# A WKV recurrence with a soft mixture of experts: scores on four quarters of the array, and the bonus sums with r*k as the stationary operand

## The chip, the cores and the metric

The kernel runs on one core of a Trainium2 chip. The metric is the device time in microseconds (us) of one execution. The engines are PE (TensorE: matmuls, with its weight loads listed apart as PEld), DVE (VectorE), ACT (ScalarE), POOL (GpSimd) and SP (SyncE, which issues the DMAs). All data is float32, and a float32 matmul stands in the trace as two weight loads and two matmuls (two passes); a transpose of float32 stands as one of each.

## The reference

A recurrence over 768 tokens for 4 batches of 8 heads of size 48, followed by a soft mixture of experts over the 3072 tokens of width 384.

```python
def _attn_ref(r, k, v, w, u):
    B, H, S, D = r.shape                      # 4, 8, 768, 48
    state = np.zeros((B, H, D, D))
    for t in range(S):
        cur = np.einsum('bhd,bhe->bhde', u[None] * kt, vt)
        y[:, :, t] = np.einsum('bhd,bhde->bhe', rt, state + cur)
        state = wt[:, :, :, None] * state + np.einsum('bhd,bhe->bhde', kt, vt)

def _moe_ref(x, phi, w1, w2):                 # 8 experts with 4 slots each
    logits = x @ phi
    d = softmax of logits over the tokens     # slot_input = d.T @ x
    slot_out[e] = np.maximum(slot_input[e] @ w1[e], 0.0) @ w2[e]
    c = softmax of logits over the slots
    return c @ slot_out
```

The term with `u` is a scalar for each token and head, a = sum over d of r*k*u, times v. The kernel computes it apart from the rest. Its tensor `rk` holds r*k with the head's rows along the partitions and the tokens along the free axis, and `u_sb` holds u in a few columns.

## The kernel before

The recurrence is cut into chunks of 128 tokens (C = 6 for a sequence). A *unit* is a load of 128 partitions: two heads of 48 rows at partitions 0 and 64, and below each of them 16 rows that are a third of a further head. Three loaded units (NU = 3) so hold the data of four pairs of heads, and the fourth pair (its rows gathered by small DMAs into `k3` and `r3`) is worked on like the others. There are 4 batches of 4 pairs, so NIT = 16 pairs, and a software pipeline runs over `it` from 0 to 16: in step `it` the pair n = it - 1 is computed, the results of pair m = it - 2 are taken from PSUM and fed to the mixture, and the scans for later units are made.

The order on each engine is that of the code (a schedule by hand). In a step PE does, one after the other:

- transposes of the keys (`tp`, L298; five matmuls, not for the fourth pair), which ACT copies to `kn` (L299, L302);
- `b_scores` (L313): for each of six chunks and each of two heads one matmul of keys against queries. The 48 rows of a head lie at array rows 0 or 64, all 128 key columns are the stationary operand, and the 128 tokens of the queries stream. It goes in two halves of three chunks. The result `ap` (a bank for each head) is copied by ACT to `at` (L317) and masked by POOL (L318);
- `d_a` (L252), in steps in which a unit is prepared (`A`, it % 4 < 3): u is stationary in three column groups of 32, and r*k streams with 256 tokens for each. The result [96, 256] is copied by ACT to `aT` (L255);
- `b_u` (L329): the chunks' contributions to the state (`up`), which DVE scans into `Sb` (L335) and ACT copies to `Sn` (L338);
- transposes of the finished results of pair m (`tp`, L384), copied by ACT to `xT` (L386), not in every step;
- `c_av` (L350): masked scores against v, with a stationary operand of 128 rows by 64 columns;
- `d_a_turn` (L260): two transposes of `aT`, so that the tokens lie along the partitions; ACT copies the result to `a` (L263);
- the mixture's logits `lp` (L401), in one step in four its sums `sp` (L448) and its transposes `dp` and `ln` (L438, L471);
- `c_inter` (L365): queries against `Sn`, on quarters of the array (48 rows by 64 columns), into the same `y` as `c_av`.

DVE does the decay scans (L206 and L218) with the products around them (L217, L220), the scan of the state (L335) and the evacuation of `y` plus `av` into `x` (L375). POOL makes `rk` (L244), the masks and `av` (L284: v times `a`, for the next step). SP loads the inputs of later units (`ld`, `rt`, `vt`) and, in pieces, the expert weights (`wt`).

The PSUM tiles of `d_a`, `d_a_turn`, the scores and the transposes come from one pool of four banks (`ps_t`, tag `tp`). Behind step 16 follow the mixture's sums and the two expert layers (L536, L572) and the output (L601).

Of the kernel before, what the change touches and what calls it, by code (L numbers as in the profile page):

```python
# [9 lines left out]
F32 = mybir.dt.float32  # L10
# [9 lines left out]
P = 128  # L20
# [21 lines left out]
NU = 3  # L42

NL = 4
PART = 16

HALF = 3

E1 = P + 1
# [4 lines left out]
def rwkv_soft_moe(ctx: ExitStack, tc: tile.TileContext, wkr, v, ublk, phi, w1, w2, out_a, out_b):  # L54
    nc = tc.nc
# [3 lines left out]
    C = v.shape[3]  # L59
# [16 lines left out]
    small = ctx.enter_context(tc.tile_pool(name="small", bufs=2))  # L76
# [13 lines left out]
    ps_t = banks.enter_context(tc.tile_pool(name="ps_t", bufs=4, space=PSUM))  # L90
# [6 lines left out]
    def a_load(i, lo=0, hi=R_OFF):  # L97
        nc.sync.dma_start(out=lds[i % NL][:, lo:hi], in_=wkr[i, :, lo:hi])

    def a_load_r(i, lo=0, hi=SCAN):  # L100
        nc.sync.dma_start(out=rts[i % NL][:, lo:hi], in_=wkr[i, :, R_OFF + lo:R_OFF + hi])
# [10 lines left out]
    ident = const.tile([P, P], F32, name="ident")  # L112
# [9 lines left out]
    NTG = 3  # L122
    TG = NTG * NS
# [3 lines left out]
    u_sb = const.tile([P, NG, 32], F32, name="u_sb")  # L127
# [34 lines left out]
    rks = [decay.tile([P, S], F32, name=f"rk{n}") for n in range(2)]  # L162
# [16 lines left out]
    def keys(i):  # L179
        return by_chunk(lds[i % NL][:, K_OFF:R_OFF])[:, :, 1:E1]  # L180
# [14 lines left out]
    parts, a3 = {}, {}  # L195
    xb = {}

    def a_load_v(i):
        vt = vpool.tile([P, 2, C, D], F32, name="vt")
        nc.sync.dma_start(out=vt, in_=v[i])  # L200
        sts[i]["vv"] = vt
# [27 lines left out]
    def a_gather(i):  # L229

        lo = PART * (i % NU)
        for dst, src in ((k3, lds[i % NL][:, K_OFF:R_OFF]), (r3, rts[i % NL])):
            for h in range(2):
                nc.sync.dma_start(out=dst[64 * h + lo:64 * h + lo + PART], in_=src[64 * h + D:64 * h + 64])

# [10 lines left out]

    def d_a(i):

        ap = ps_t.tile([TG, 2, P], F32, name="aps", tag="tp")
        rkc = rks[i % 2].rearrange("p (c e) -> p c e", e=P)  # L250
        for j in range(NTG):
            nc.tensor.matmul(out=ap[32 * j:32 * j + 32], lhsT=u_sb[:, i % NU, :], rhs=rkc[:, j:C:NTG, :],  # L252
                             start=True, stop=True)
        parts[i] = aT = small.tile([TG, 2, P], F32, name="aT", bufs=1)
        nc.scalar.copy(out=aT, in_=ap)  # L255

    def d_a_turn(i):
        tp = ps_t.tile([P, 2, P], F32, name="atp", tag="tp")
        for n in range(2):
            nc.tensor.transpose(out=tp[:, n, 0:TG], in_=parts[i][:, n, :], identity=ident[0:TG, 0:TG])  # L260

        parts[i] = a = small.tile([P, 4, C, 1], F32, name="a", bufs=5)
        nc.scalar.copy(out=a.rearrange("p h (n j) o -> p h n (j o)", n=2),  # L263
                       in_=tp[:, :, 0:TG].rearrange("p n (j q) -> p q n j", q=32)[:, 0:4])

    def d_a_last(b):
        a3[b] = t = small.tile([P, 2, C, 1], F32, name="a3")
# [4 lines left out]
    def unit(i):  # L272
        return NU * (i // NG) + i % NG

    def rows_of(i):
        if i % NG == NU:
            return k3, r3
        return lds[unit(i) % NL][:, K_OFF:R_OFF], rts[unit(i) % NL]
# [7 lines left out]
    def b_kn(i, hf):  # L286
# [6 lines left out]
        kn, kv = st["kn"], keys(unit(i))  # L293
        at3 = PART * (i % NG)
        lo, hi = ((0, 3), (3, C - 1))[hf]
        tp = ps_t.tile([P, 3, P], F32, name="tp")
        for c in range(lo, hi):
# [4 lines left out]
        nc.scalar.copy(out=bass.AP(tensor=dst.tensor, offset=dst.offset + at3,  # L302
                                   ap=[dst.ap[0], dst.ap[1], [64, 2], [1, PART]]), in_=src)

    def b_scores(i, hf):
        st = sts[i]
        kt_, rt_ = rows_of(i)
        aps = [ps_t.tile([P, 3, P], F32, name="ap", tag="tp") for _ in range(2)]
        order = [(cc, h) for cc in range(3) for h in range(2)]
        for cc, h in order:  # L310
            c = 3 * hf + cc
            rows = slice(64 * h, 64 * h + D)
            nc.tensor.matmul(out=aps[h][:, cc, :], lhsT=kt_[rows, c * E1 + 1:(c + 1) * E1],  # L313
                             rhs=rt_[rows, c * E1:c * E1 + P], start=True, stop=True)
        for h in range(2):
            at = work.tile([P, 3, P], F32, name="at")
            nc.scalar.copy(out=at, in_=aps[h])  # L317
            nc.gpsimd.affine_select(  # L318
                out=at, in_=at, pattern=[[0, 3], [1, P]], compare_op=ALU.is_gt,
                fill=0.0, base=0, channel_multiplier=-1)  # L320
            st["AT", h, hf] = at
# [291 lines left out]
    def recompute():  # L613
# [5 lines left out]
        with tc.tile_pool(name="f_dram", bufs=1, space=DRAM) as f_dram, \  # L619
# [17 lines left out]
            with tc.For_i(0, B, 1) as ib:  # L637
              for g in range(NG):
                for h in range(2):
# [186 lines left out]
    for it in range(NIT + 1):  # L826
        n, m = it - 1, it - 2
        ph = it % NG
        A, i = it < NIT and ph < NU, unit(it)
        B_ = n >= 0  # L830
        mb, mg = divmod(m, NG)
        X = m >= 0 and mg >= 1
        Y = mg == 0 and mb >= 1
        Z = mg == 1 and mb >= 1
        U_ = B_ and n % NG < NU

        done = i if it == 0 or (A and ph) else unit(it + 1) if ph == NU and it + 1 < NIT else None
        if U_:
            a_gather(unit(n))
        if 1 <= it < NIT - 1:  # L840
            a_load_v(it + 1)
        if m >= 0 and m % NG < NU and unit(m) + NL < NSC:
            a_load(unit(m) + NL)
            a_load_r(unit(m) + NL)
        if it < NIT:
            more_weights(it)
        if it == NIT:
            early.close()
            late = weights.enter_context(tc.tile_pool(name="late", bufs=1, side="right", reuse_waits="tile"))
            w_b = weights.enter_context(tc.tile_pool(name="w_b", bufs=N_WB, side="right", reuse_waits="tile"))  # L850
            load_weight(w_b, wts, N_WB)
            cT = late.tile([P, NT // NB, P], F32, name="cT")
            siT = late.tile([P, E * KT, NS], F32, name="siT")
            nc.gpsimd.memset(siT, 0.0)
        if it == 0:
            masks()
            d_rk(0)
            scans(0, (("G", 0), ("F", 0), ("G", 1), ("F", 1)))
            d_a(0)
            d_a_turn(0)  # L860
            keep_warm(N_WARM_2[0], ps_t, "tp")
            d_rk(1)
        if ph == NU:
            d_a_last(it // NG)
        if B_:
            d_av(n)
            b_kn(n, 0)
            if n:
                b_kn(n, 1)
            b_scores(n, 0)  # L870
            if not n:
                keep_warm(N_WARM_2[1], ps_t, "tp")
                b_kn(n, 1)
        if m >= 0:
            c_evac(m)
        if it != 1:
            pieces_of(it, FIRST)
        if B_:
            b_scores(n, 1)
        if A and it:  # L880
            d_a(i)
        if B_:
            b_u(n)
        if Y:
            s_exp(mb - 1, qs[mb - 1])
        if X:
            xT = l_turn(xb[mb], mg - 1, once, ps_t)
            if mg == 1:
                lts[mb] = small.tile([TG, 2, P], F32, name="lt", bufs=1)
        if B_:  # L890
            if not U_:
                spread(pat3, k3)
            b_state(n)
        if Z:
            s_norm(mb - 1, qs[mb - 1])
        if it == 1:
            d_rk(2)
            pieces_of(it, FIRST)
        pieces_of(it, SECOND)

        if ph == NU - 1 and it + 2 < NIT:
            d_rk(i + 1)
        elif ph == NU and it + 1 < NIT:
            d_rk(done + 1)
        elif A and ph == 0 and it:
            d_rk(i + 2)
        if it == 1:
            keep_warm(N_WARM_2[2], ps_t, "tp")
        if B_:
            c_y(n)  # L910
            c_av(n, 0)
            c_av(n, 1)
        if A and it:
            d_a_turn(i)
        if X:
            l_part(mg - 1, xT, lts[mb], ps_t)
        if done is not None:
            a_pat(done)
            a_end(done)
        if X and mg == NG - 1:  # L920
            qs[mb] = s_max(mb, lts[mb], cst[0:TG, 2:3])
        if Y:
            s_dturn(qs[mb - 1], ps_t)
            s_rows(qs[mb - 1], ps_t)
            s_rows_exp(qs[mb - 1])
        if Z and mb < B - 1:
            s_slots(xb[mb - 1], mb - 1, qs[mb - 1], ps_t)
        if it == 1:
            keep_warm(N_WARM_2[3], ps_t, "tp")
        if B_:  # L930
            c_inter(n, 0)
            c_inter(n, 1)
        if Z and mb < B - 1:
            s_sum(mb - 1, qs[mb - 1])
# [21 lines left out]
    q = s_max(lb, lp)  # L956
# [162 lines left out]
```

## Time and profile before

| | |
|---|---|
| median of three runs | 188.88 us (186.36, 188.88, 191.8) |
| profiled execution, time of its own | 189.19 us |
| its span | 187.4 us |
| mean granted TensorE clock | 0.975 |
| PE, DVE, ACT, POOL busy | 88%, 65%, 48%, 41% |

The steps of the recurrence fill the span from about 6 to 136 us; the expert layers and the output take the rest. A group row of the profile gives the line, the engine and the operation, output<-inputs, shapes and count, then the busy time and the mean duration of one, then the idle time ahead of it and what ended that. Matmuls of different parts of the array overlap, so the time of a run of them is read from the chain of waits or the timeline, not from the mean of one. "issue" is idle time that ended on nothing that the trace shows.

### The profile page before, as it was taken

How to read it: one execution, taken by the hardware profiler on the slowest of the kernel's cores; microseconds unless marked ns; L12 is line 12 of the kernel's file. 1: busy time of each engine (PE TensorE's matmuls, PEld its weight loads, DVE VectorE, ACT ScalarE, POOL GpSimd, SP SyncE). 2: the span in 40 equal slices, each digit the busy share in tenths (PEclk: the TensorE clock that was granted, in tenths of full speed). 3: DMA queues.
4: the chain of work that ended last, by engine and by line, in shares of the span. 5: the costliest groups of instructions: out<-in, count | busy, mean ns of one | idle time of the engine just before them, and what ended most of it. 6: DMA issues, size and time to landing. Idle time of an engine off the chain costs nothing.

```text
span 187.4 us, 7253 instructions
## 1 busy us (share of the span) xinstructions
PE 165.8 (88%) x3000; PEld 116.6 (62%) x3000; DVE 121.5 (65%) x237; ACT 90.8 (48%) x266; POOL 76.5 (41%) x133
## 2 busy tenths in 40 slices
PE   7499979799999889999899999899789999999710
PEld 2166758677878758688777787787554324755510
DVE  5599978867897977989799889731335222033520
ACT  3054547455677726667765586784450002022430
POOL 3357286572448567445577643557004000000000
PEclk9999999969999999999999999999999999999985
DMA  5999599995779999389999259497999159907692
GB/s 148 339 396 358 116 388 328 357 406 193 230 224 366 323 397 346 75 238 319 299 368 390 53 169 285 117 330 249 418 320 415 73 167 415 417 17 294 261 385 94
DMA packets 14249, 51.93 MB, mean 277 GB/s; under 512 B 2304, under 2 KB 3200, under 8 KB 13568
## 3 DMA queue, kind: packets, MB, share of 16 engines
q1 hardware_dynamic: 14208, 51.38, 77.3%
q8 instruction: 26, 0.43, 0.9%
q14 instruction: 15, 0.12, 0.2%
HBM read 44.28 MB, written 4.72 MB: 261 GB/s over the span
## 4 chain that ended last, share of the span: by engine, by line
PE 48%; DVE 27%; DMA 7%; ACT 7%; issue 5%; POOL 1%; SPq 0%; ACTq 0%; DVEq 0%; POOLq 0%
PE ap L313 9%; DVE cst L218 6%; PE hp L536 6%; PE so L572 6%; DVE cst L206 5%; DMA rt<-in_wkr_dram 5%; PE y L365 5%; DVE Sb L335 4%; DVE ld L217 3%; PE tp L384 3%; PE op L601 3%; PE up L329 3%; ACT Sn L338 3%; PE tp L298 3%; PE sp L448 3%
## 5 line engine op out<-in xcount | busy, mean ns | idle before, releaser
L318 POOL TENSOR_SCALAR_AFFINE_SELECT at<-at 128x384 f32<-128x384 f32 x64 | 31.2, 523 | 28.7 <-ACT at L317 28.7
L317 ACT COPY at<-ap 128x384 f32<-128x384 f32 x64 | 26.4, 490 | 6.8 <-PE ap L313 5.6
L350 PE MATMUL y<-vt,at 128*64 128x48 f32 x768 | 25.5, 223 | 0.0
L350 PEld LDWEIGHTS y<-vt,at 128*64 128x64 f32 x768 | 23.7, 138 | 2.3 <-POOL at L318 1.7
L284 POOL TENSOR_TENSOR av<-vt,a 128x576 f32<-128x576 f32 x16 | 18.5, 1154 | 13.7 <-ACT a L263 13.7
L218 DVE TENSOR_TENSOR_SCAN cst<-ld,cst 128x387 f32<-128x387 f32 x24 | 23.2, 968 | 0.8
L313 PE MATMUL ap<-rt,ld 48*128 48x128 f32 x288 | 22.8, 286 | 0.7 <-issue 0.7
L206 DVE TENSOR_TENSOR_SCAN cst<-ld,cst 128x387 f32<-128x387 f32 x24 | 22.9, 953 | 0.8 <-DMA ld<-in_wkr_dram 0.6
L244 POOL TENSOR_TENSOR rk<-rt,ld 128x384 f32<-128x384 f32 x24 | 20.3, 868 | 7.3 <-DMA rt<-in_wkr_dram 4.1
L313 PEld LDWEIGHTS ap<-rt,ld 48*128 48x128 f32 x288 | 20.1, 187 | 2.2 <-issue 1.3
L335 DVE TENSOR_TENSOR_SCAN Sb<-up,pat 112x288 f32<-112x288 f32 x16 | 12.1, 753 | 11.9 <-ACT pat L224 7.4
L375 DVE TENSOR_TENSOR x<-y,av 128x576 f32<-128x576 f32 x16 | 12.1, 756 | 8.9 <-PE y L365 8.9
L338 ACT COPY Sn<-Sb 112x240 f32<-112x240 f32 x16 | 10.1, 629 | 12.2 <-DVE Sb L335 12.2
L386 ACT COPY xT<-tp 128x384 f32<-128x384 f32 x24 | 10.3, 482 | 9.0 <-PE tp L384 9.0
L217 DVE TENSOR_TENSOR ld<-ld,cst 128x387 f32<-128x387 f32 x24 | 13.0, 542 | 2.2 <-POOL rk L244 2.2
L365 PE MATMUL y<-Sn,rt 48*64 48x48 f32 x480 | 10.1, 222 | 4.6 <-ACT Sn L338 2.7
L365 PEld LDWEIGHTS y<-Sn,rt 48*64 48x64 f32 x480 | 8.4, 134 | 9.4 <-issue 3.6
L299 ACT COPY kn<-tp 128x336 f32<-128x336 f32 (+1 forms) x24 | 9.6, 401 | 8.9 <-PE tp L298 8.7
L220 DVE TENSOR_TENSOR rt<-rt,cst 128x387 f32<-128x387 f32 x24 | 13.4, 558 | 0.8
L329 PEld LDWEIGHTS up<-vt,kn 128*48 128x48 f32 x320 | 8.8, 128 | 7.0 <-issue 5.8
L572 PE MATMUL so<-wt,hT 128*32 128x208 f32 (+1 forms) x256 | 12.5, 329 | 0.0
L384 PE MATMUL tp<-ident,x 128*128 128x128 f32 x72 | 10.9, 289 | 1.0 <-DVE x L375 1.0
(130 smaller groups left out, 241.9 us busy)
## 6 DMA issues: line engine op xcount, KB each, us to landing
wt<-in_w_dram SPq DMA_DIRECT2D x24, 512.0 KB, 7.1
ld<-in_wkr_dram SPq DMA_DIRECT2D x11, 775.0 KB, 6.4
wt<-in_w_dram SPq DMA_DIRECT2D x5, 1536.0 KB, 9.0
vt<-in_v_dram SPq DMA_DIRECT2D x16, 288.0 KB, 4.9
rt<-in_wkr_dram SPq DMA_DIRECT2D x11, 387.0 KB, 5.9
wt<-in_w_dram SPq DMA_DIRECT2D x3, 832.0 KB, 6.4
out_dram<-wt SPq DMA_DIRECT2D x3, 832.0 KB, 3.9
wt<-in_w_dram SPq DMA_DIRECT2D x3, 704.0 KB, 10.1
```

The lines of the kernel that those rows point to most:

```text
L206: nc.vector.tensor_tensor_scan(out=prod[:, ::-1], data0=t[:, lo + 1:lo + 1 + HALF * E1][:, ::-1], data1=one, initial=1.0, op0=ALU.mult, op ...
L217: nc.vector.tensor_tensor(out=k_, in0=k_, in1=prod, op=ALU.mult)
L218: nc.vector.tensor_tensor_scan(out=prod, data0=lds[i % NL][:, lo:lo + HALF * E1], data1=big, initial=1.0, op0=ALU.mult, op1=ALU.min)
L244: nc.gpsimd.tensor_tensor(out=rks[i % 2].rearrange("p (c e) -> p c e", e=P)[:, part], in0=queries(i)[:, part], in1=keys(i)[:, part], op=AL ...
L284: nc.gpsimd.tensor_tensor(out=av, in0=st["vv"], in1=a.broadcast_to([P, 2, C, D]), op=ALU.mult)
L313: nc.tensor.matmul(out=aps[h][:, cc, :], lhsT=kt_[rows, c * E1 + 1:(c + 1) * E1], rhs=rt_[rows, c * E1:c * E1 + P], start=True, stop=True)
L317: nc.scalar.copy(out=at, in_=aps[h])
L318: nc.gpsimd.affine_select(out=at, in_=at, pattern=[[0, 3], [1, P]], compare_op=ALU.is_gt, fill=0.0, base=0, channel_multiplier=-1)
L335: nc.vector.tensor_tensor_scan(out=Sb[0:ROWS].rearrange("p e n -> p (e n)"), data0=up[0:ROWS].rearrange("p e n -> p (e n)"), data1=(pat3 i ...
L350: nc.tensor.matmul(out=st["y"][cols, h, c * D:(c + 1) * D], lhsT=st["AT", h, hf][:, cc, cols], rhs=st["vv"][:, h, c, :], start=(c == 0), s ...
L365: nc.tensor.matmul(out=st["y"][cols, h, c * D:(c + 1) * D], lhsT=t[rows, c * E1 + 64 * th:c * E1 + 64 * th + 64], rhs=Sn[rows, c - 1, :], ...
L572: nc.tensor.matmul(out=so[32 * g:32 * g + NS, :], lhsT=hT[ft // 2][:, ft % 2, e, :], rhs=wts[E + e][:, base + ft * wd:base + (ft + 1) * wd ...
```

## The change

Scores: each matmul's stationary operand is cut into two halves of 64 columns, so that a matmul takes 48 rows by 64 columns of the array (a quarter) and writes 64 of the 128 partitions of its bank. The 128 tokens of the queries stream as before, now twice for each chunk and head. There are 24 matmuls in a step in place of 12.

Sums: r*k becomes the stationary operand, in pieces of 64 tokens, and four columns of u stream. The result has the tokens along the partitions at once, so `d_a_turn` and the copy to `aT` go, and `a` is copied in `d_a`. There are 12 matmuls in place of 3, and no transposes.

```diff
     def d_a(i):
 
-        ap = ps_t.tile([TG, 2, P], F32, name="aps", tag="tp")
-        rkc = rks[i % 2].rearrange("p (c e) -> p c e", e=P)
-        for j in range(NTG):
-            nc.tensor.matmul(out=ap[32 * j:32 * j + 32], lhsT=u_sb[:, i % NU, :], rhs=rkc[:, j:C:NTG, :],
-                             start=True, stop=True)
-        parts[i] = aT = small.tile([TG, 2, P], F32, name="aT", bufs=1)
-        nc.scalar.copy(out=aT, in_=ap)
-
-    def d_a_turn(i):
...
+        ap = ps_t.tile([P, C, 4], F32, name="aps", tag="tp")
+        for c in range(C):
+            for th in range(2):
+                nc.tensor.matmul(out=ap[HP * th:HP * th + HP, c, :],
+                                 lhsT=rks[i % 2][:, c * P + HP * th:c * P + HP * th + HP],
+                                 rhs=u_sb[:, i % NU, 0:4], start=True, stop=True)
         parts[i] = a = small.tile([P, 4, C, 1], F32, name="a", bufs=5)
-        nc.scalar.copy(out=a.rearrange("p h (n j) o -> p h n (j o)", n=2),
-                       in_=tp[:, :, 0:TG].rearrange("p n (j q) -> p q n j", q=32)[:, 0:4])
+        nc.scalar.copy(out=a.rearrange("p h c o -> p c (h o)"), in_=ap)
...
-        order = [(cc, h) for cc in range(3) for h in range(2)]
-        for cc, h in order:
+        for cc, th, h in [(cc, th, h) for cc in range(3) for th in range(2) for h in range(2)]:
             c = 3 * hf + cc
             rows = slice(64 * h, 64 * h + D)
-            nc.tensor.matmul(out=aps[h][:, cc, :], lhsT=kt_[rows, c * E1 + 1:(c + 1) * E1],
+            k0 = c * E1 + 1 + HP * th
+            nc.tensor.matmul(out=aps[h][HP * th:HP * th + HP, cc, :], lhsT=kt_[rows, k0:k0 + HP],
                              rhs=rt_[rows, c * E1:c * E1 + P], start=True, stop=True)
...
-        if A and it:
-            d_a_turn(i)
```

On PE, in the step of the fourth pair of a batch, the row is this before (line, instruction, output<-inputs, columns of the stationary by columns of the moving operand, and how many in a row):

```order
L365 MATMUL y<-Sn,rt_103 64x48 x20
L313 MATMUL ap<-r_138,k_137 128x128 x12
L252 MATMUL aps<-rk_134,u_sb 32x256 x3
L329 MATMUL up<-vt,kn_139 48x48 x10
L384 MATMUL tp<-ident,x 128x128 x6
L350 MATMUL y<-vt,at 64x48 x24
L260 MATMUL atp<-ident,aT 128x96 x2
L401 MATMUL lp<-xT,phi_sb 32x256 x3
L365 MATMUL y<-Sn,r_138 64x48 x20
```

And this now, with the lines of the changed file (seven lower from `b_scores` on):

```order
L358 MATMUL y<-Sn,rt_103 64x48 x20
L306 MATMUL ap<-r_138,k_137 64x128 x24
L253 MATMUL aps<-u_sb,rk_134 64x4 x12
L322 MATMUL up<-vt,kn_139 48x48 x10
L377 MATMUL tp<-ident,x 128x128 x6
L343 MATMUL y<-vt,at 64x48 x24
L394 MATMUL lp<-xT,phi_sb 32x256 x3
L358 MATMUL y<-Sn,r_138 64x48 x20
```

The scores have 24 rows in place of 12 and the sums 12 in place of 3; the two transposes between `c_av` and the logits are gone, and nothing else has moved.

On ACT, the next step (a first pair of a batch) reads thus before:

```order
L317 COPY at<-ap 128x384 x4
L255 COPY aT<-aps 96x256
L386 COPY xT<-tp 128x384 x2
L338 COPY Sn<-Sb 112x240
L263 COPY a<-atp 128x24
L224 COPY pat_136<-ld_100 128x48x5
```

And thus now:

```order
L310 COPY at<-ap 128x384 x4
L257 COPY a<-aps 128x6x4
L379 COPY xT<-tp 128x384 x2
L331 COPY Sn<-Sb 112x240
L225 COPY pat_136<-ld_100 128x48x5
```

The copy to `a` has moved from behind `Sn` to the place of the copy to `aT`, which is gone. The instructions of DVE, POOL and SP are the same in number and order.

More of the change, by code (lines that the diff above doesn't have):

```diff
@@ L45 @@
 PART = 16
+HP = P // 2
 HALF = 3
@@ L247, in d_a @@
     def d_a(i):
-        ap = ps_t.tile([TG, 2, P], F32, name="aps", tag="tp")
-        rkc = rks[i % 2].rearrange("p (c e) -> p c e", e=P)
-        for j in range(NTG):
-            nc.tensor.matmul(out=ap[32 * j:32 * j + 32], lhsT=u_sb[:, i % NU, :], rhs=rkc[:, j:C:NTG, :],
-                             start=True, stop=True)
-        parts[i] = aT = small.tile([TG, 2, P], F32, name="aT", bufs=1)
-        nc.scalar.copy(out=aT, in_=ap)
-    def d_a_turn(i):
-        tp = ps_t.tile([P, 2, P], F32, name="atp", tag="tp")
-        for n in range(2):
-            nc.tensor.transpose(out=tp[:, n, 0:TG], in_=parts[i][:, n, :], identity=ident[0:TG, 0:TG])
+        ap = ps_t.tile([P, C, 4], F32, name="aps", tag="tp")
[4 more added lines that the diff above has]
+                                 rhs=u_sb[:, i % NU, 0:4], start=True, stop=True)
         parts[i] = a = small.tile([P, 4, C, 1], F32, name="a", bufs=5)
-        nc.scalar.copy(out=a.rearrange("p h (n j) o -> p h n (j o)", n=2),
-                       in_=tp[:, :, 0:TG].rearrange("p n (j q) -> p q n j", q=32)[:, 0:4])
+        nc.scalar.copy(out=a.rearrange("p h c o -> p c (h o)"), in_=ap)
     def d_a_last(b):
@@ L859, in rwkv_soft_moe @@
             d_a(0)
-            d_a_turn(0)
             keep_warm(N_WARM_2[0], ps_t, "tp")
```

## The prediction

> **What bounds the kernel now.** The page first: its engine line, its two lines by slices of 4.7 us, the instruction queue, and the shares of the chain of waits.
>
> ```profile
> PE 165.8 (88%) x3000; PEld 116.6 (62%) x3000; DVE 121.5 (65%) x237; ACT 90.8 (48%) x266; POOL 76.5 (41%) x133
> PEclk9999999969999999999999999999999999999985
> DMA  5999599995779999389999259497999159907692
> q8 instruction: 26, 0.43, 0.9%
> PE 48%; DVE 27%; DMA 7%; ACT 7%; issue 5%; POOL 1%; SPq 0%; ACTq 0%; DVEq 0%; POOLq 0%
> ```
>
> PE carries the chain, DVE comes second, and PE has by far the most instructions: 6000 of about 6640. "q8" brought 26 packets of 0.43/26 MB = 16.5 kB. The third thing to see is the 5% of "issue", idle time that nothing in the trace ends. So I read the timeline of PE at such a hole, and then the counts of instructions from hole to hole (view by stretches; matmuls and weight loads counted apart).
>
> ```profile
> 36.27 0.45 PE L365 MATMUL y<-Sn,rt 48*64 48x48 f32 x15 [1.21 <-issue]
> 62.76 0.27 PE L313 MATMUL ap<-rt,ld 48*128 48x128 f32 x1 [0.71 <-issue]
> 69.20 0.32 PE L365 MATMUL y<-Sn,rt 48*64 48x48 f32 x5 [0.68 <-issue]
> 99.82 1.41 PEld L313 LDWEIGHTS ap<-r,k 48*128 48x128 f32 x22 [0.29 <-issue]
> 130.14 0.27 PE L313 MATMUL ap<-r,k 48*128 48x128 f32 x1 [0.43 <-issue]
> ...
> core 0: us, PE busy (x) PEld busy (x) DVE busy (x) ACT busy (x) POOL busy (x), PEclk, DMA share, GB/s
> 36.26:62.76 26.50, 25.25 (x501) 20.41 (x502) 21.28 (x37) 17.19 (x53) 13.84 (x23) 0.94 0.84 291
> 62.76:69.18 6.42, 5.75 (x128) 3.95 (x127) 5.82 (x13) 3.17 (x8) 4.37 (x7) 1.00 1.01 371
> 69.18:99.82 30.64, 29.74 (x626) 23.61 (x626) 26.59 (x48) 19.74 (x58) 17.92 (x29) 1.00 0.84 283
> 99.82:130.13 30.31, 29.10 (x628) 23.98 (x629) 21.91 (x40) 20.55 (x62) 16.30 (x29) 1.00 0.67 216
> ```
>
> The holes stand in the middle of runs of equal matmuls (after 25 of 40, after 35 of 40, ahead of the last of 24), so no semaphore explains them. Between them lie 1003, 255, 1252 and 1257 instructions: 4, 1, 5 and 5 times 256, less some semaphore instructions that the counts leave out. [...] I read this as PE running out of instructions: at every 256th the next packet has to be there. When is it asked for? The DMA view of two stretches behind such a boundary, one under load, one not (the second boundary is found by counting 256 on from 69.18):
>
> ```profile
> q1 hardware_dynamic: 392, 1.45, 99.1%
> ...
> q8 instruction: 1, 0.02, 5.8%
> ...
> 69.18:76.04 6.86, 6.60 (x124) 5.10 (x126) 5.40 (x8) 3.96 (x10) 3.61 (x7) 1.00 0.86 314
> ...
> q8 instruction: 1, 0.02, 5.9%
> ```
>
> The first row is 62.76 to 66.85: the DMA engines are full and no instruction packet moves. The second is 66.85 to 67.9: there it is, and PE goes on at 69.20, 1.3 us behind it. The boundary at 76.04 finds a quiet queue: its packet lies between 77.0 and 78.0 (last row). So a packet is asked for when the one before is opened, and takes 69.20 - 62.76 = 6.4 us under load, some 2.0 + 1.3 = 3.3 us without. 93.91 to 99.82 is 256 instructions and one more fetch that was waited for: 5.9 us.
>
> ```profile
> 93.91:99.82 5.91, 5.82 (x134) 4.08 (x130) 5.71 (x12) 3.17 (x7) 4.57 (x8) 1.00 1.00 375
> ```
>
> [...]
>
> **The change part by part.** The direct terms come from these rows, of the chain in order of time and of the groups:
>
> ```profile
> 44.50 0.80 PE y L365 x40
> 45.30 0.70 PE tp L298 x5
> 46.00 1.75 PE ap L313 x24
> 47.75 0.56 PE aps L252 x6
> 48.31 0.61 PE up L329 x20
> ...
> 64.42 1.53 PE y L350 x48
> ...
> 145.37 2.71 PE hp L536 x24
> ...
> L350 PEld LDWEIGHTS y<-vt,at 128*64 128x64 f32 x768 | 23.7, 138 | 2.3 <-POOL at L318 1.7 <-issue 0.6
> L313 PEld LDWEIGHTS ap<-rt,ld 48*128 48x128 f32 x288 | 20.1, 187 | 2.2 <-issue 1.3 <-ACT ce L481 0.5 <-ACT kn L302 0.2
> L260 PE MATMUL atp<-ident,aT 96*128 96x96 f32 x24 | 4.6, 274 | 0.5 <-ACT aT L255 0.5
> L255 ACT COPY aT<-aps 96x256 f32<-96x256 f32 x12 | 4.6, 380 | 7.1 <-PE aps L252 7.1
> L263 ACT COPY a<-atp 128x24 f32<-128x24 f32 x12 | 2.1, 175 | 3.4 <-PE atp L260 3.4
> ```
>
> *Scores on quarters.* L536 streams 512 columns on four column groups, one per 2.71/24 = 113 ns, so a group needs 4 x 113 = 452 ns, 0.88 ns a column, and 128 columns need 113 ns. The scores before are 12 rounds of two: 12 x 0.113 = 1.36 us, and two starts of some 0.2 us make the 1.75. After the change they are 12 rounds of four, and that four quarters do run at once is seen in L365 (0.80/40 = 20 ns each, for 48 columns that stream 42 ns). The rounds stay at 113 ns, so nothing is won in the stream. What is won is the first weight load of each half, 187 - 138 = 0.05 us, of which one half a step is free (the other waits for ACT's copies of `kn` to clear a bank), and, in the four steps without L298, the empty 0.15 us between L365 and the scores, which now have the same shape: 16 x 0.05 + 4 x 0.15 = 1.4 us, two thirds of it on the chain: -0.9.
>
> *Sums.* 12 matmuls are 24 passes with a stationary operand like that of L350, 1.53/48 = 32 ns each: 0.77 us for 0.56, +0.2 us in eleven steps, less some 0.07 for the shape that L329 shares. The chain passes L252 in four of them: +0.5. `rk` from POOL is due at the same place as before.
>
> *The turn that goes.* Two transposes, about 0.3 us of PE with their start, stand behind L350, where PE goes on to wait for `Sn` (the row below: 6.6 us in 8 times). They are hidden, and gain nothing now; if PE comes late they are 0.3 us of slack. Should that cover go, the price is 11 x 0.3 = 3.3 us at most. ACT loses the copy of 380 ns; it is busy 48% and no `Sn` waits for it: hidden. `a` is ready earlier by the stretch from L252 to L260, which ends POOL's wait for it; `av` is needed only a step later by L375: nothing. The bank of `atp` comes free, and banks only turn sooner. SP's queue holds the same DMAs.
>
> ```profile
> PEld y L365 <- ACT Sn L338: 6.6, 8, 1.5
> ...
> 20.00:56.00 36.00, 33.27 (x686) 26.56 (x686) 29.77 (x51) 21.43 (x63) 18.65 (x32) 0.95 0.83 285
> 56.00:76.00 20.00, 18.04 (x391) 14.20 (x391) 16.91 (x30) 12.18 (x36) 13.00 (x22) 1.00 0.96 345
> 84.00:104.00 20.00, 19.35 (x410) 15.53 (x401) 18.53 (x36) 13.71 (x42) 13.54 (x24) 1.00 0.93 330
> 121.00:136.00 15.00, 13.26 (x321) 11.01 (x313) 4.71 (x9) 9.03 (x25) 7.29 (x12) 1.00 0.89 321
> ```
>
> *More instructions.* Scores add 24 passes a step, so 48 instructions; the sums add 36 and the turn takes 4 away. In 16 steps that is 16 x 48 + 12 x 32 = 1152 on 6000, all of them between 10 and 135 us, where they are a quarter more: 4.5 packets. Under load (the 9s of the DMA line) lie about 19 us from 23 to 42, and the last three rows. From 56 to 76 PE has 782 instructions; two steps' scores (96), one of sums (36) and two turns (-8) make 906, 3.5 packets, in the 20 - 1.4 = 18.6 us that it runs: 5.2 us a packet. The two rows below it give 4.9 (212 more instructions) and 5.1 (96 more) in the same way. The supply is 6.4 and 5.9, say 6.2: each packet fetched under load comes 1.2 us late. About 14 packets are opened there, and the fetch of the first in each of the four stretches starts in a short queue: 10 x 1.2 = 12 us of holes. The five holes before are 3.3 us. More holes: 8.7 us.
>
> Not all of them are on the path. With three packets in two steps, the boundaries fall in turn into L365, L350 and L313. A hole in L350 first eats the wait for `Sn`, 6.6/8 = 0.8 us, and the 0.3 us of the turn: 3.3 holes lose 1.1 each, 3.6 us. So 8.7 - 3.6 = +5.1. From below it is nothing (every hole meets a wait), from above 8.7. I take 4.9: the 5.1, less a little for a hole that falls where DVE has the chain (27% of it).
>
> Sum: -0.9 + 0.5 + 4.9 = +4.5 us on the profiled execution's 189.19: 193.7. That execution lies 0.3 above the median of the runs shown (188.88), so the forecast is 193.4.
>
> **The rivals.**
> - *The holes are covered.* They would have to meet PE's waits for `Sn` or DVE's scans three times in four: 8.7/4 - 0.4 = +1.8, so 190.7. For it speaks that DVE has 27% of the chain; against it that all five holes shown lie inside L313 and L365, where PE waits for nothing else. It decides where less than 4.2 us of the 8.7 get through: then it is not slower.
> - *Fetches are hidden after all*: the holes have another cause that more instructions don't multiply. Then the direct terms stand alone, 188.88 - 0.4 = 188.5. For it speaks that only 5 of the 26 packets are followed by a hole, against it the multiples of 256. [...]
> - *Quarters stream faster.* Were the 113 ns of a round set by the load of 128 columns and not by the stream, a round would drop to L365's 4 x 20 = 80 ns: 12 x 0.033 = 0.4 us a step, 16 steps, -6 us, and with the holes at their lower end 182.5. L536 speaks against it: its weight loads have 32 columns, and a column still costs 0.88 ns.
> - *The clock.* The one 6 in PEclk, at 37 to 42 us, follows the longest hole (1.21 us). A second such stretch, of longer holes, would cost about 2 us more, and the holes at their upper end with it: 189.2 + 8.7 + 2 = 199.9.
>
> **How the numbers follow.** Late packets on the path as priced: 0.48. Covered holes: 0.28. Fetches hidden: 0.11. Faster quarters: 0.06. The clock as well: 0.07. About 2% (3.8 us) is what a measurement of this kernel can tell from no change. So slower is 0.48 + 0.07 = 0.55, the same 0.28 + 0.11 = 0.39, faster 0.06. The time is the likeliest case's, 193.4. The range reaches from the case with hidden fetches, 188.5, to the holes' upper end, 189.2 - 0.4 + 8.7 = 197.5; outside lie the two last rivals and half of the hidden case, together under 0.2. The forecast's own range is 192.0 to 197.5.
>
> **What would show it.** In the changed profile: PE and PEld with some 3576 instructions each and "q8" with about 30 packets; the score runs of 48 in about 1.7 us; `aps` with 24 in 0.7 to 0.8; no `atp`; and in the waits of PE and PEld, "issue" rows in the middle of L306, L343 and L358, 256 instructions apart, of about 1 us each and some 12 us together. If those rows stay near 3.3 us, the fetch is not what I think, and the time stays near 188.5. If they grow and the time doesn't, the waits for `Sn` must have shrunk by as much. If the score runs fall under 1.4 us, my reading of the stream is wrong.

## The result and the profile after

| | before | after |
|---|---|---|
| median of four runs each (lowest, highest), us | 188.28 (186.36, 191.8) | 196.55 (194.27, 201.78) |
| profiled execution, its own time | 189.19 | 194.27 |
| its span | 187.4 | 192.6 |
| its mean granted TensorE clock | 0.975 | 0.966 |

The changed kernel is slower: ratio 1.0432, 95% interval 1.0307 to 1.0557. (Comparisons leave out disturbed runs, so a ratio is not always the quotient of the two medians.)

The page of the changed kernel: its span, the engines, the granted clock in slices of 4.8 us, the instruction queue, the shares of the chain.

```profile
span 192.6 us, 8385 instructions
...
PE 166.8 (87%) x3576; PEld 120.9 (63%) x3576; DVE 121.4 (63%) x237; ACT 88.3 (46%) x254; POOL 76.2 (40%) x133
...
PEclk9999995799999999999999999999999999999985
...
q8 instruction: 30, 0.49, 1.1%
...
PE 59%; DVE 15%; DMA 9%; issue 6%; ACT 5%; SPq 1%; ACTq 0%; DVEq 0%
```

PE has its 576 matmuls and 576 weight loads more and is busy only 1.0 us longer; q8 (the queue of the instruction packets) brought four packets more. "issue" went from 5% to 6% of the chain. The half-clock stretch (5 and 7 in PEclk; a granted clock of 0.50 from 29.1 to 35.9 us) is longer than the single 6 of before (0.50 from 38.0 to 41.4 us).

To see where the 5.2 us of span came from, I cut both executions at three rows that mean the same thing in both: a run of the state's part of `y` (L365, now L358) at about 52 us, the last such run, and the last copy of the output to `wt`. From the timelines, before first:

```profile
core 0 of [0], span 187.4 us
...
52.04 0.74 PE L365 MATMUL y<-Sn,rt 48*64 48x48 f32 x36
...
134.41 0.80 PE L365 MATMUL y<-Sn,r 48*64 48x48 f32 x40 [0.52 <-ACT Sn L338]
...
179.34 0.34 DVE L609 COPY wt<-op 128x176 f32<-128x176 f32 x1
```

The same rows after:

```profile
core 0 of [0], span 192.6 us
...
51.99 0.56 PE L358 MATMUL y<-Sn,rt 48*64 48x48 f32 x24
...
137.85 0.80 PE L358 MATMUL y<-Sn,r 48*64 48x48 f32 x40 [0.53 <-ACT Sn L331]
...
182.78 0.34 DVE L602 COPY wt<-op 128x176 f32<-128x176 f32 x1
```

| stretch | before | after | difference |
|---|---|---|---|
| start to the step at 52 us | 52.04 | 51.99 | -0.1 |
| from there to the last step | 82.37 | 85.86 | +3.5 |
| last step to the last copy (expert layers) | 44.93 | 44.93 | 0.0 |
| last copy to the end of the span | 8.06 | 9.82 | +1.8 |

Up to 52 us the two are even: before had a hole of 1.21 us and a half-clock stretch of 3.4 us there, after a half-clock stretch of 6.8 us and no hole. The 3.5 us come from the steps behind it, where both have full clock until the last copy, and 1.8 us come from the exit, when all arithmetic is over.

What PE waited for between 52 and 142 us (view of waits: total us, times, longest), before:

```profile
PE y L365 <- ACT Sn L338: 2.4, 6, 0.5
PE ap L313 <- issue: 1.1, 2, 0.7
...
PE y L365 <- issue: 0.7, 1, 0.7
```

And after:

```profile
PE y L358 <- issue: 3.0, 4, 1.3
PE y L358 <- ACT Sn L331: 2.9, 4, 0.9
PE y L343 <- issue: 2.5, 2, 1.5
```

"issue" was 1.1 + 0.7 = 1.8 us and is 3.0 + 2.5 = 5.5 us: 3.7 more, the size of the 3.5 us. The waits for `Sn` did not shrink in return (2.4, now 2.9). The six holes stand in the middle of runs of equal matmuls, as the timeline of PE shows:

```profile
52.91 0.45 PE L358 MATMUL y<-Sn,rt 48*64 48x48 f32 x16 [0.35 <-issue]
...
58.50 1.25 PE L343 MATMUL y<-vt,at 128*64 128x48 f32 x36 [1.06 <-issue]
...
69.69 0.44 PE L358 MATMUL y<-Sn,rt 48*64 48x48 f32 x13 [0.77 <-issue]
...
100.44 0.55 PE L358 MATMUL y<-Sn,rt 48*64 48x48 f32 x19 [0.58 <-issue]
...
106.58 0.61 PE L343 MATMUL y<-vt,at 128*64 128x48 f32 x14 [1.47 <-issue]
...
131.68 0.44 PE L358 MATMUL y<-Sn,rt 48*64 48x48 f32 x14 [1.25 <-issue]
```

And the stretches from hole to hole:

```profile
core 0: us, PE busy (x) PEld busy (x) DVE busy (x) ACT busy (x) POOL busy (x), PEclk, DMA share, GB/s
52.89:69.69 16.80, 14.96 (x377) 11.98 (x378) 14.41 (x28) 10.67 (x31) 10.30 (x17) 1.00 0.96 336
69.69:100.43 30.74, 28.77 (x757) 23.66 (x756) 26.63 (x49) 19.44 (x57) 17.78 (x30) 1.00 0.84 283
100.43:106.57 6.14, 4.67 (x125) 4.08 (x125) 5.20 (x10) 3.50 (x10) 4.37 (x8) 1.00 0.60 232
106.57:131.67 25.10, 22.92 (x631) 19.30 (x632) 16.12 (x31) 15.26 (x46) 11.46 (x20) 1.00 0.63 196
```

PE and PEld together issue 755, 1513, 250 and 1263 instructions: 3, 6, 1 and 5 times 256, less the few that the counts leave out, and in these stretches q8 brings 3, 6, 1 and 5 packets. The holes stand on packet edges, as before.

When the packets land can be read as well (view of DMA, in windows of 0.02 us). The six holes end at 52.91, 58.50, 69.69, 100.44, 106.58 and 131.68 us, and a packet of q8 lands at 50.58, 55.84, 67.26, 98.06, 104.22 and 129.26 us: 2.3 to 2.7 us ahead of each. The holes of before, its five shown ahead, end 2.3 to 2.5 us behind a packet. So each hole ends much the same time behind a packet, whatever its own length, which is what waiting for that packet looks like.

### The profile page after: what moved, and what is told of

The parts are those of the page before. It is cut to its first block, busy times and chain, and to the rows that moved or that the text cites. A ratio compares the mean times of both kernels' runs of the same rounds, so it can differ in the third digit from the quotient of the medians.

```text
span 192.6 us, 8385 instructions
## 1 busy us (share of the span) xinstructions
PE 166.8 (87%) x3576; PEld 120.9 (63%) x3576; DVE 121.4 (63%) x237; ACT 88.3 (46%) x254; POOL 76.2 (40%) x133
## 4 chain that ended last, share of the span: by engine, by line
PE 59%; DVE 15%; DMA 9%; issue 6%; ACT 5%; SPq 1%; ACTq 0%; DVEq 0%
PE ap L306 11%; DMA ld<-in_wkr_dram 7%; PE y L343 6%; PE y L358 6%; PE hp L529 6%; PE so L565 6%; PE tp L377 4%; PE up L322 4%; DVE cst L219 3%; PE aps L253 3%; PE tp L291 3%; DVE cst L207 3%; PE op L594 3%; PE sp L441 2%; DVE Sb L328 2%
## 5 line engine op out<-in xcount | busy, mean ns | idle before, releaser
L310 ACT COPY at<-ap 128x384 f32<-128x384 f32 x64 | 27.1, 485 | 9.6 <-PE ap L306 8.3
L343 PE MATMUL y<-vt,at 128*64 128x48 f32 x768 | 27.0, 227 | 2.5 <-issue 2.5
L343 PEld LDWEIGHTS y<-vt,at 128*64 128x64 f32 x768 | 24.8, 141 | 5.2 <-issue 4.2
L306 PE MATMUL ap<-rt,ld 48*64 48x128 f32 x576 | 23.3, 290 | 0.6 <-ACT kn L295 0.6
L306 PEld LDWEIGHTS ap<-rt,ld 48*64 48x64 f32 x576 | 18.7, 139 | 4.1 <-PE tp L291 1.3
L358 PE MATMUL y<-Sn,rt 48*64 48x48 f32 x480 | 10.8, 223 | 6.4 <-ACT Sn L331 3.4
L358 PEld LDWEIGHTS y<-Sn,rt 48*64 48x64 f32 x480 | 8.8, 134 | 11.2 <-issue 5.5
L253 PEld LDWEIGHTS aps<-u_sb,rk 128*64 128x64 f32 x288 | 9.6, 137 | 3.8 <-POOL rk L245 1.6
```

What stands on the lines that cost most here:

```text
L306: nc.tensor.matmul(out=aps[h][HP * th:HP * th + HP, cc, :], lhsT=kt_[rows, k0:k0 + HP], rhs=rt_[rows, c * E1:c * E1 + P], start=True, stop ...
L343: nc.tensor.matmul(out=st["y"][cols, h, c * D:(c + 1) * D], lhsT=st["AT", h, hf][:, cc, cols], rhs=st["vv"][:, h, c, :], start=(c == 0), s ...
L358: nc.tensor.matmul(out=st["y"][cols, h, c * D:(c + 1) * D], lhsT=t[rows, c * E1 + 64 * th:c * E1 + 64 * th + 64], rhs=Sn[rows, c - 1, :], ...
```

## The experiments

Two theories carry most of them. *A, the supply*: PE waits at packet edges because packets come late while the weights and inputs are loaded; the more instructions, the more such waits. *A', the exit*: the 1.8 us at the end are a packet edge too, one that falls among PE's last instructions behind the branch over a block that is not run here (`if` on the input's range, in which the recurrence would be computed another way). The rivals are told in each expectation. Lines of the kernels are those of their own files.

**One part of the change alone.** Before with the scores on quarters and the old sums:

```diff
-        for cc, h in order:
+        for cc, th, h in [(cc, th, h) for cc in range(3) for th in range(2) for h in range(2)]:
...
+            k0 = c * E1 + 1 + HP * th
+            nc.tensor.matmul(out=aps[h][HP * th:HP * th + HP, cc, :], lhsT=kt_[rows, k0:k0 + HP],
                              rhs=rt_[rows, c * E1:c * E1 + P], start=True, stop=True)
```

> The kernel before with the scores on quarters alone, the sums as before: 768 more PE instructions, exactly 3 packets of 256. Theory A (PE runs out of instructions under DMA load): holes ('issue' rows inside L313, L350 and L365 and their like) grow from 3.3 us to 5 to 9 us, the last start of the state's part of y moves from 134.4 us to 136 to 138.5, the time by +2 to +5 us (ratio 1.01 to 1.027). Rival B (the cost is the direct time of the new matmuls and drains): a run of 48 score matmuls takes as long as one of 24 did, so no change or -1 us. Rival C (the sums are the whole loss): no change.

Measured: median 191.65 us against 187.96 for before (ratio 1.0173, 1.0086 to 1.026). In the profile the last step starts at 137.36 us (134.41 before) and the exit takes 8.6 us. The waits of PE from 20 to 142 us that bear on it:

```profile
PE y L351 <- issue: 1.2, 2, 0.8
PE sp L449 <- issue: 1.1, 1, 1.1
PE ap L314 <- ACT at L318: 1.1, 1, 1.1
...
PE y L366 <- issue: 0.7, 1, 0.7
PE ap L314 <- issue: 0.7, 2, 0.4
```

The step at about 52 us starts at 51.7, and all these holes lie behind it: from there the steps take 85.7 us against 82.4, 3.3 more, nearly as much as in after. "issue" is 3.7 us in six holes, 1.9 more than before; a further 1.1 us stands at a packet edge as well (79.3 us), where the view names ACT's copy of `at`. So the scores alone carry the loss in the steps, and the holes account for most of it. A had 2 to 5 us more time and the last step at 136 to 138.5 us, and both came so; its 5 to 9 us of holes did not quite (3.0 before, now 3.7, or 4.8 with the one at 79.3 us).

The other part, before with the new sums and the old scores:

```diff
+        ap = ps_t.tile([P, C, 4], F32, name="aps", tag="tp")
+        for c in range(C):
+            for th in range(2):
+                nc.tensor.matmul(out=ap[HP * th:HP * th + HP, c, :],
+                                 lhsT=rks[i % 2][:, c * P + HP * th:c * P + HP * th + HP],
+                                 rhs=u_sb[:, i % NU, 0:4], start=True, stop=True)
...
-        if A and it:
-            d_a_turn(i)
```

> The kernel before with the new sums alone, the scores as before: 384 more PE instructions, 1.5 packets. Theory A: one and a half more packets in the steps cost +1 to +2 us, the 0.1 us longer run of the sums +0.5 us, and the odd half packet puts a packet's edge among PE's last instructions behind the branch, as in the changed kernel: +1.7 us at the exit (from the last matmul to the end 9.3 us in place of 7.6). Together +3 to +4 us. Rival B (direct time): +0.5 to +1.5 us in the steps, nothing at the exit. Rival C (the sums are the whole loss): +5 to +8 us.

Measured: median 193.27 us (189.57 to 197.77) against 187.96; no ratio was formed. In the profiled execution, of 189.57 us, the steps lost nothing: the last one starts at 132.82 us, 82.0 behind the step at about 52 us (82.4 before), with 1.9 us of holes from 20 us on (3.0 before). But the exit took 187.9 - 177.75 = 10.15 us. So in this profile the sums add no wait in the steps, where A had forecast 1 to 2 us for their one and a half packets (a miss), and what they cost shows at the exit, which is tried below.

**The number of instructions by itself.** Before, with 24 tiny bfloat16 matmuls (48 instructions) a step into columns of `y` that nothing reads:

```diff
+            for q in range(24):
+                j = 32 * (q % 4)
+                nc.tensor.matmul(out=sts[n]["y"][j:j + 32, 0, 400:401], lhsT=zb[:, 0, j:j + 32], rhs=zb[:, 0, 0:1],
+                                 start=False, stop=False)
```

> The kernel before with 24 tiny bf16 matmuls a step (32 rows of zeros by one column, into columns of y that nothing reads, on four column groups) ahead of the matmuls that wait for Sn: 768 more PE instructions, as many as the quarters bring, and next to no work (0.2 to 0.4 us a step, where PE waits for Sn 0.8 us anyway in half of the steps). Theory A: +2 to +5 us, with holes of 5 to 9 us at multiples of 256 instructions, as with the quarters themselves. Rival B: the quarters or the sums cost something of their own that this does not have: 0 to +1.5 us and holes as before, 3.3 us.

Measured: median 198.42 us against 187.96 (ratio 1.0426, 1.0324 to 1.0527). That is far above both expectations. Its clock line and one run of the added matmuls:

```profile
PEclk9999995797599859999999999999979999999975
```

```profile
97.93 0.31 PE L933 MATMUL y<-zb 128*32 128x1 bf16 x24
```

The added run takes 0.31 us, 16 of them 5 us, and the clock was halved four times up to 149 us, for 23.8 us together. The holes in the steps were 4.3 us, below the 5 to 9 of A. The run doesn't isolate the count, since the half clock and the added runs' own time came with it, and it is left as inconclusive for A.

**The load taken away.** A says that without the weights' transfers the added instructions cost nothing. The 24 pieces of the expert weights are all issued in step 15 in place of steps 2 to 15, in before and in after; only the steps ahead of that one are then read:

```diff
-PER_IT = (0, 0, 2, 2, 2, 1, 2, 2, 2, 1, 2, 2, 2, 1, 2, 1)
+PER_IT = (0, 0, 0, 0, 0, 0, 0, 0, 0, 0, 0, 0, 0, 0, 0, 24)
```

> The kernel before with all 24 pieces of early expert weights (12.6 of the 31 MB that move during the steps) asked for in the last step instead of spread over them: the DMA engines are far less loaded during the steps, the expert layers then wait for their weights, so only the steps are read. Theory A: an instruction packet takes 3 to 4 us, the holes at multiples of 256 instructions fall from 3.3 us to under 1 us, and the last run of the state's part of y starts 1 to 5 us sooner than 134.4 us. Rival (the holes do not hang on the DMA load): they stay at 3 us or more.

> The changed kernel with the same late weights. Theory A: with packets of 3 to 4 us and 5 us of work in each, the holes fall from 7 us to under 1.5 us, and the last run of the state's part of y starts within 1 us of where it starts in the kernel before with late weights (the original two stand 3.4 us apart). Rival B (the new matmuls cost time of their own): they stay 2.5 to 4 us apart.

The starts of four steps and the holes, late weights in before:

```profile
51.84 0.80 PE L365 MATMUL y<-Sn,rt 48*64 48x48 f32 x40
58.67 0.80 PE L365 MATMUL y<-Sn,rt 48*64 48x48 f32 x40 [0.33 <-ACT Sn L338]
...
125.24 0.80 PE L365 MATMUL y<-Sn,rt 48*64 48x48 f32 x40
...
131.85 0.80 PE L365 MATMUL y<-Sn,r 48*64 48x48 f32 x40 [0.52 <-ACT Sn L338]
```

Late weights in after:

```profile
51.28 0.80 PE L358 MATMUL y<-Sn,rt 48*64 48x48 f32 x40
58.42 0.80 PE L358 MATMUL y<-Sn,rt 48*64 48x48 f32 x40 [0.71 <-ACT Sn L331]
...
125.29 0.56 PE L358 MATMUL y<-Sn,rt 48*64 48x48 f32 x24
...
127.42 0.45 PE L358 MATMUL y<-Sn,rt 48*64 48x48 f32 x16 [1.57 <-issue]
...
134.20 0.67 PE L343 MATMUL y<-vt,at 128*64 128x48 f32 x14 [1.93 <-issue]
...
135.35 0.80 PE L358 MATMUL y<-Sn,r 48*64 48x48 f32 x40
```

Up to the second-last step the two kernels are 0.05 us apart; with the weights spread over the steps they were 129.77 - 127.33 = 2.4 apart at the same place. Ahead of 52 us each has 1.3 us of holes and one half-clock stretch of 3.4 us. From there to 125 us neither has a hole, where with the weights in their old places before had 1.4 us of them and after 4.2 up to the same step; the DMA share from 52 to 100 us is 0.58 and 0.57 in place of 0.88 and 0.87. The 0.05 us are in part luck: between the steps at 52 and 125 us the changed kernel takes 125.29 - 51.28 = 74.01 us and before 125.24 - 51.84 = 73.40, so 0.6 us is its own cost without any hole, made up for ahead of 52 us.

In after the weights are asked for from 118.7 us on. In the last step, into which they fall, after has two holes of 1.57 and 1.93 us (2.3 and 2.6 us behind a packet), and the kernels part by 3.5 us. The expectation named the last run, and there the letter of rival B (2.5 to 4 us) is met; but the kernels part only once the weights move. The holes of before were expected to fall to under 1 us; 1.3 us are left, all ahead of 52 us. Times as a whole are of no use here (207.71 and 206.9 us), since the experts wait for their weights. With one profile of each, this is the strongest evidence for A: without the weights' transfers the added instructions cost 0.6 us in ten steps, and the holes come where the weights run beside them (DMA share from 52 to 100 us 0.87 in place of 0.57).

**The load made even.** If the holes come from load, it should help to spread it. Here the steps with little other input carry two or three pieces and those in which a unit is loaded one:

```diff
-PER_IT = (0, 0, 2, 2, 2, 1, 2, 2, 2, 1, 2, 2, 2, 1, 2, 1)
+PER_IT = (0, 0, 1, 1, 1, 3, 1, 1, 1, 3, 1, 1, 3, 3, 2, 2)
```

> The kernel before with the weight pieces moved from the steps that also load inputs to the steps that load none (per step 0,0,1,1,1,3,1,1,1,3,1,1,3,3,2,2 in place of 0,0,2,2,2,1,2,2,2,1,2,2,2,1,2,1): the same bytes, spread more evenly. Theory A: shorter waits for packets, holes of 0.5 to 2.5 us in place of 3.3, and a time 1 to 3 us shorter (ratio 0.984 to 0.995). Rival: the late pieces make the expert layers wait, or the holes stay: 0 to +3 us.

> The changed kernel with the weight pieces spread in the same way. Theory A: it gains more than the kernel before does, since more packets are fetched under load: 2 to 5 us off the changed kernel's 196.5 us, 191.5 to 194.5 (ratio 1.018 to 1.035 to the kernel before). Rival B: it gains no more than the kernel before does from the same move (0 to 2 us).

Measured: medians of 187.39 us for before with even loads and 197.33 us for after with even loads (193.06 to 200.87), against 189.02 for before; no ratio was formed. For before the holes from 20 us on add to 3.0 us, as many as without the move, where A had 0.5 to 2.5. For after A had 191.5 to 194.5 us, and the median missed it. Its executions with a clock of 0.965 and 0.973 took 194.27 and 193.06 us, and those of after with 0.951 to 0.967 took 194.27 to 196.86, so a small gain is not excluded. The profile is that of the longest execution (200.87 us, clock 0.918); its clock line and its waits from 20 to 142 us:

```profile
PEclk9999999757999999999879999658999999999965
```

```profile
PE y L343 <- POOL av L277: 2.9, 1, 2.9
PE ap L306 <- issue: 2.4, 2, 1.3
PE y L358 <- issue: 2.0, 1, 2.0
PE y L343 <- issue: 0.8, 2, 0.6
```

5.2 us of "issue", as much as in after, a wait of 2.9 us that after does not have (at a packet edge too, at 125.6 us, though the view names POOL), and three half-clock stretches in the steps in place of one. In these two profiles moving the load moved the holes and did not lessen them. The median of before with even loads lay 1.6 us below that of before, so it ran once more, unchanged:

> The kernel before with the evenly spread weight pieces once more, now with five rounds, as the version that might beat both: theory A gives 0.5 to 2.5 us less than the kernel before (ratio 0.987 to 0.997); the rival, that its holes stay (4.4 us of gaps in the first look, against 4.8), gives 0.995 to 1.005.

Median 189.84 us against 188.4 (ratio 1.0195, 1.0086 to 1.0305): no gain. Nothing that ran beats the kernel before.

**The exit.** If A' is right, the exit depends on where the packet edges fall behind the branch, and code that is never run moves them. After, with 8 matmuls (16 instructions) more in that block:

```diff
+                for _ in range(2):
+                    nc.tensor.matmul(out=vb[0:ROWS, 0, 0:1], lhsT=zb[:, 0, 0:ROWS], rhs=zb[:, 0, 0:1],
+                                     start=True, stop=True)
```

> The changed kernel with eight more matmuls in the block that recomputes everything and is never run: nothing executed changes, but the code behind that block moves by 16 instructions. Theory A': the 1.7 us by which the changed kernel takes longer from its last matmul to its end (9.3 us in place of 7.6) is a packet's edge between PE's last instructions; moved by 16 it is gone, and the end stage takes 7.5 to 7.9 us. Rival: the end stage is longer for another reason (the branch, the loads, the output's DMA), and stays at 9.3 us. Time against the kernel before: +2 to +5 us by the theory, +4 to +8 by the rival.

The same edit on the kernel with the new sums alone:

> The new sums alone, with 16 more instructions in the block that is never run. Theory A': the exit is 1.5 to 2 us shorter than with the new sums alone. Theory A: 1.5 packets more in the steps cost 0 to 2 us, so the time is -1 to +2 us against the kernel before (ratio 0.995 to 1.01). Rival C (the sums are a good part of the loss): ratio 1.015 or more.

And before with 64 of them (`range(16)`, 128 instructions), to bring the edge to where before has none:

> The kernel before with 64 more matmuls (128 instructions) in the block that is never run, which is the half packet by which the changed kernel's length differs from its own. Theory A': a packet's edge now falls among PE's last instructions, and the stretch from the last matmul to the end grows by 1.5 to 2 us, with the steps unchanged. Rival (the exit hangs on something else in the changed kernel): it stays at 7.5 to 7.7 us from the last work on.

The last copy in the three timelines, in this order:

```profile
core 0 of [0], span 192.9 us
...
184.82 0.34 DVE L602 COPY wt<-op 128x176 f32<-128x176 f32 x1
```

```profile
core 0 of [0], span 188.5 us
...
180.30 0.34 DVE L602 COPY wt<-op 128x176 f32<-128x176 f32 x1
```

```profile
core 0 of [0], span 189.1 us
...
178.45 0.34 DVE L609 COPY wt<-op 128x176 f32<-128x176 f32 x1
```

From the last copy to the end: 8.1 us in after with the 16 instructions (9.8 without), 8.2 with the sums alone and the 16 (10.15 without), 10.65 in before with the 128 (8.1 without). Code that no engine runs so takes away 1.7 and 2.0 us, and adds 2.6 (A' had 1.5 to 2). The scores alone, whose 768 instructions are three whole packets (q8 has 29 in place of 26), left the exit at 8.6 us. That the place of the code sets it is shown. That it is a packet which is waited for is argued: every one of these traces has a last instruction packet some 7 us behind the last copy, at 189.94 us in after. The span ends 2.7 us behind it in after and 3.1 and 3.3 us in the two other long exits, about what PE needs behind a packet in the steps (2.3 to 2.7 us); in the short exits it ends 0.9 to 1.2 us behind it (before: packet at 186.48, end at 187.4), too soon to have waited for it.

In whole times: after with the 16 instructions 197.07 us against 187.96 (ratio 1.0395, 1.0296 to 1.0493), which is not told apart from after itself; its profile had a half-clock stretch of 10.2 us in the steps, and its last copy came 2.0 us later than in after. The sums alone with the 16: 188.22 against 188.4 (ratio 1.0104, 0.9972 to 1.0237), no difference that can be measured. Before with the 128: 189.7 against 188.4 (ratio 1.0208, 1.0021 to 1.0396).

## Why the prediction was right, and where its sizes were not

The forecast was 193.4 us with a range of 188.5 to 197.5, slower the likeliest; the median of 196.55 lies in the range's upper half. The mechanism held, in that PE waits for packets (each hole ends 2.3 to 2.7 us behind one) and the waits for `Sn` take up a part; the sizes of both terms were wrong in opposite directions, and two things outside the sum came on top. That the profiled executions differ by 5.1 us, and the sum had 4.5, is therefore partly luck.

- *Counts and direct terms.* 3576 matmuls, 30 packets: as forecast. No row gives the number of instructions in a packet, by which the sum was priced; from hole to hole of before, with 1003, 255, 1252 and 1257 instructions, q8 brings 4, 1, 5 and 5 packets, so 256 to a packet is an estimate from these counts. From the chain after, in order of time:

```profile
70.13 1.72 PE ap L306 x48
71.85 0.83 PE aps L253 x24
```

  The score run was to take about 1.7 us and takes 1.72 (1.75 before): quarters stream no faster here than halves. The sums were to take 0.7 to 0.8 and take 0.83. The direct terms came to -0.4 in the sum; with the weights out of the way the changed kernel takes 0.6 us more from 52 to 125 us, so over these steps they were small, and of the other sign.
- *The turn* was to gain nothing, since its 0.3 us are hidden in the wait for `Sn`. The late weights agree with that: the five waits for `Sn` from 52 to 125 us are 0.33, 0.24, 0.54, 0.24 and 0.55 us in before and 0.71, 0.52, 0.86, 0.55 and 0.94 in after, each 0.3 to 0.4 longer. With the sums alone the steps from 52 us on took 82.0 us in one profile and 83.6 in the other, against 82.4 before, so two profiles of the same executed code differ by more than this.
- *More holes, 8.7 us*: the step that was mis-sized. The sum had ten packets late by 1.2 us each, 12 us in all. From 52 us on there are six holes, 0.35 to 1.47 us, 5.5 in all, and 3.7 more than before. In the first of the four stretches that the sum took as loaded, 23 to 42 us, there is none, so over all the steps the holes grew by 2.5 us (3.0 to 5.5). A fetch under load was as slow as taken (100.43 to 106.57 us are 256 instructions and the next packet: 6.1 us, with a hole of 1.47 at their end), but of the two stretches on either side, with 6 and 5 packets, only the last one in each came visibly late. I had taken whole stretches of high DMA share as load for each packet in them; I read this as a packet competing only with what is queued when it is asked for. The 6.1 us fit that (DMA share 1.02 up to 103.00 us and 0.30 behind it, packet at 104.22), but no run tested it by itself.
- *3.6 us of it hidden* behind the waits for `Sn`: right in kind, far too large. The two holes in L343 (1.06 and 1.47 us) did eat the waits behind them: in after the runs at 60.16 and 108.44 us start without a wait for `Sn`, where the same runs with late weights wait 0.71 and 0.55 us, and the other three waits are the same in both to 0.01 us (0.53, 0.87, 0.93). So two holes lost some 1.3 us, not 3.3 holes 1.1 each. The 0.8 us per wait of the sum was the idle time of the weight loads (PEld: 6.6 us in 8 times); PE itself waited 3.9 us in 8 times, 0.5 each. That the waits as a whole grew from 2.4 to 2.9 us goes with the turn, which no longer fills them. Of the 8.7 - 3.6 = 5.1 that were forecast, 3.5 came: too many holes and too much hiding made up for each other in part.
- *The exit, +1.8 us*, was in no term. It would follow from the same mechanism, and the count of instructions that I had would have told that the last edges move; I only counted those in the steps.
- *The clock* was a rival with a chance of 0.07, as a second half-clock stretch behind longer holes. In the profile the stretch only grew, from 3.4 to 6.8 us, and there it is balanced by a hole that before has. But the profile is the fastest of the four runs of after, with a clock of 0.966; the other three had 0.951, 0.956 and 0.923, and took 196.23, 196.86 and 201.78 us. Two further executions took 195.63 us with 0.967 and 205.55 us with 0.903. Before was at 0.975 in its profile. The medians differ by 8.3 us and the profiled executions by 5.1; the 3.2 us between them go in part with these lower clocks. That is argued from the runs' clocks and times, since only one execution has a trace, and the execution at 0.967 was 1.4 us longer than the profile's without a lower clock. What lowers the clock is open.
- *Fetches hidden* fell. With the weights late no hole shows from 52 to 125 us, and about a fifth more instructions cost 0.6 us; with the weights spread over the steps there are 5.5 us of holes from 52 us on. (The prediction read the packet behind the edge at 62.76 us as landing 1.3 us ahead of PE's restart; it landed at 66.88, 2.3 us ahead.)

## What to carry to other kernels

Count a tiling's instructions as well as its columns: cutting a stationary operand in two doubles them, and where the array streams no faster (48 in 1.72 us against 24 in 1.75) there is only the cost. Where "issue" stands inside runs of equal instructions, look whether the distances are multiples of one number (here 256, less a few) with a whole number of instruction packets in each; if so, look whether each ends at the same distance behind a packet (here 2.3 to 2.7 us). Here fewer instructions (1.8 us of such holes from 52 us on in before, 5.5 in after) and fewer transfers (none from 52 to 125 us with late weights) each meant fewer such holes; spreading the same transfers differently did not (3.0 us from 20 us on in before, with even loads too). Price such edges one by one, by what is queued when the packet is asked for (a reading that no run tested by itself), and remember those at the end of the program.

## What the hardware showed that was not expected

The length of a block that is never run moved the end of the execution by 1.7 to 2.6 us (exit of 8.1 us or 9.8 us in after, 8.1 or 10.65 in before), with all arithmetic the same. A change of 16 instructions in such a block so looked like a change of 1% (1.7 us) in the executed code.

The half clock often began within two microseconds of a long idle time of PE: at 38 us in before (hole of 1.21 us ending at 36.3), at 37.1 us in after with the 16 instructions (hole of 1.41 us ending at 36.7), and in after with even loads at 37.1, 98.6 and 125.9 us (holes of 2.03, 1.34 and 2.89 us ending at 37.1, 97.1 and 125.6). In the steps it lasted 3.4 us in before, 6.8 in after and 10.2 in after with the 16 instructions. But holes of 1.06 to 1.47 us in after, and one of 1.57 us with late weights, had no such sequel, and the stretch at 29.1 us in after has no hole ahead of it, only a wait of 1.62 us for `Sn` that ended at 27.7. So a late packet may cost several times its own length, and when it does was not settled.
